# Block-causal attention and a feed-forward layer on one core: the last query and key blocks turned in the PSUM bank of the scores

## The chip, the cores and the metric

The kernel runs on one core of a Trainium2 chip. Its engines are TensorE (PE in the profile, with its weight loads as PEld), VectorE (DVE), ScalarE (ACT), GpSimd (POOL) and SyncE (SP, which here only issues DMAs). Each engine works through its own instructions in order, and they wait for each other through semaphores. The metric is the device time of one launch in microseconds; the time shown is a median of three runs.

## The reference

Attention over 8 batches of 8 heads with 576 positions of 64 columns each. A query may look at keys of its own block of 64 and of earlier blocks. The heads of a batch are then put side by side as rows of 512 columns, and a feed-forward layer with a clipped quadratic in its middle follows. All tensors are float32.

```
scores = scale * np.matmul(q, k.transpose(0, 1, 3, 2))
mask = block_i >= block_j                  # blocks of 64 positions
scores = np.where(mask, scores, -1000000000.0)
attn = np.exp(scores - np.max(scores, axis=-1, keepdims=True))
attn = attn / (np.sum(attn, axis=-1, keepdims=True) + 1e-09)
attn_out = np.matmul(attn, v)

x = attn_out.transpose(0, 2, 1, 3).reshape(B * S, H * D)     # 4608 x 512
h = x @ w_in                                                  # 512 x 2048
g = np.where(h >= 1, h, np.where(h <= -1, 0.0, (h + 1) ** 2 / 4))
out = g @ w_out
```

## The kernel before, in words

Every product is made of float32r words: each operand is split into a high and a low word, and the products of words are summed in PSUM.

**Attention** goes by pairs of heads (`Pair`, 32 of them, four per batch). A head has 4.5 tiles of 128 queries: tiles 0 to 3 and a last block of 64. The last blocks of the two heads of a pair are handled together. For a head `j`, `scores(j, 0)` does query tiles 0 and 1, `scores(j, 1)` tile 2 (128 queries by 384 keys) and `scores(j, 2)` tile 3 (by 512 keys); `scores_last` does the last block of both heads. Each of these multiplies on TensorE (L484 and L487), takes the maximum of a row on VectorE (L508), the exponential on ScalarE (L513, with a read of the row sums behind it), then the sum plus a small number, the reciprocal and the scaling on VectorE (L494, L495, L519). The scaled tile `pr` then goes through a DMA into `prr` (L251), is transposed on TensorE (`turn`, L559) and split into two words by ScalarE and VectorE (L552, L554). `attn_v` multiplies with the values (L598), `add_words` adds its two halves with ScalarE and VectorE (L620, L621), and `store_x` writes the rows for the feed-forward layer (L663, L664).

From batch 2 on (`raw`, 24 pairs) queries and keys are loaded as they are and transposed together: `turned_raw` for tiles 0 to 3 of one head (L403), `turned_last` for the last blocks of both heads (L444). `parted` then makes the words: ScalarE writes the high words of the queries (L390), VectorE the low ones (L391), ScalarE those of the keys (L396), VectorE the rest (L397). `turned_last` copies the blocks to `qa` and `ka` by two more VectorE instructions (L448).

**The feed-forward layer** is interleaved, one half step after each of the eight steps of a pair: `ffn_in` has 12 matmuls of 512 columns into one PSUM bank `ph` (L777), then ScalarE (L786), VectorE (L787, L790), ScalarE (L791) and GpSimd (L792); `ffn_out` has 12 matmuls with the other weights (L801, L806).

**PSUM.** There are eight banks: four for the sums `po`, one for `ph` and three that `work_bank` hands out in turn to everything else. In the pairs from batch 2 on there are 22 such requests a pair, so a bank is used again at the third request after it, and its next writer waits until its last reader is done. The requests around the change are `scores(0, 0)`, `attn_v_first`, `turn(1, 2)` of the pair before, `scores(0, 1)`, `turned_last`, `attn_v(1)` of the pair before, `scores(0, 2)`, `turn(0, 0)` and the two banks of `scores_last`. `turned_last` thus gets the bank that `attn_v_first` had, whose last reader is the second L621 of that step.

The order on each engine is laid down when the program is built, by a scheduler that keeps close to the order of the code but may let instructions of different engines' queues pass each other.

Of the kernel before, what the change touches and what calls it, by code (L numbers as in the profile page):

```python
# [9 lines left out]
F32R = mybir.dt.float32r  # L10
# [13 lines left out]
def block_attn_then_ffn(  # L24
# [9 lines left out]
    nc = tc.nc  # L34
    B, H, S, D = q.shape
    NT, DM = out.shape
    DF = w_in.shape[1]
    P = 128
    BLK = 64
    NTL = S // P  # L40
# [5 lines left out]
    TCH = 512  # L46
# [5 lines left out]
    SCALE = 1.0 / float(D) ** 0.5  # L52
# [25 lines left out]
    def work_bank(name):  # L78

        banks["n"] += 1  # L80
        if banks["free"] and banks["n"] % 2:
            return ps_o.tile([P, 512], F32, tag="po", name=name)
        return ps_w.tile([P, 512], F32, tag="work", name=name)
# [4 lines left out]
    ident_r = const.tile([P, P], F32R, tag="ident", name="ident_r")  # L88
# [13 lines left out]
    qa = const.tile([P, 2, QW], F32R, tag="qa", name="qa")  # L102
    qb = const.tile([P, 2, QW], F32R, tag="qb", name="qb")
    ka = const.tile([P, 2, S], F32R, tag="ka", name="ka")
    kb = const.tile([P, 2, S], F32R, tag="kb", name="kb")

    def last_blocks(t_):

        view = t_[:, :, SM : SM + BLK]
        if t_.shape[2] == S:  # L110
            return view
        part, (_, two), cols = view.ap
        return bass.AP(tensor=view.tensor, offset=view.offset, ap=[part, [QW + BLK, two], cols])
# [120 lines left out]
    def as_float32r(src, plain):  # L234

        if plain:
            wide = src.shape[1] > RING - 2 * S
            places = SPARE_WIDE if wide else SPARE
            moved = [places[spare[wide] % len(places)]]
            spare[wide] += 1  # L240
            if src.shape[1] > TCH:
                if "end" not in spare:
                    spare["end"] = att1.tile([P, G0 + P], F32R, tag="pa11", name="pre")[:, :BLK]
                moved.append(spare["end"])
            for i, dst in enumerate(moved):
                n = min(TCH, src.shape[1] - i * TCH)
                nc.sync.dma_start(dst[:, :n].bitcast(F32), src[:, i * TCH : i * TCH + n])
            return moved
        n, moved = src.shape[1], []
        wide = wide_tile(F32R, "prr")  # L250
        nc.sync.dma_start(wide[:, :n].bitcast(F32), src)  # L251
        for c0 in range(0, n, TCH):
            moved.append(wide[:, c0 : min(c0 + TCH, n)])
        return moved


    class Pair:
# [157 lines left out]
        def turned(self, is_q, j):  # L415
# [18 lines left out]
            else:  # L434
                nc.sync.dma_start(
                    a[:D, j, :SM].bitcast(F32), bt[hi0 : hi0 + D, j, :SM].bitcast(F32)
                )

        def turned_last(self):

            ps = work_bank("ps_qk")
            if self.raw:
                ps = ps[:, :P]
                nc.tensor.transpose(ps.bitcast(F32R), self.qk[:, 2 * NTL, :, :], ident_r)  # L444
                ps = ps.rearrange("p (h c) -> p h c", h=2)
                self.parted(last_blocks, ps)
                for i, a in enumerate((qa, ka)):
                    nc.vector.tensor_scalar_mul(  # L448
                        last_blocks(a)[:D], ps[i * D : (i + 1) * D], 1.0 if i else SCALE
                    )  # L450
                return
            for i, src in enumerate((self.qs, self.ks)):
                nc.tensor.transpose(
                    ps[:, i * P : (i + 1) * P].bitcast(F32R), src[:, 2 * NTL, :, :], ident_r
                )
            for i, (a, bt, hi0) in enumerate(((qa, qb, 0), (ka, kb, D))):
                blocks = ps[:, i * P : (i + 1) * P].rearrange("p (h c) -> p h c", h=2)
                nc.scalar.copy(last_blocks(bt), blocks)
                nc.vector.tensor_copy(last_blocks(a)[:D], blocks[hi0 : hi0 + D])
# [34 lines left out]
                nc.vector.tensor_scalar_add(total[:, i : i + 1], total[:, i : i + 1], EPS)  # L494
            nc.vector.reciprocal(total, total)  # L495

        def scores(self, j, g):
            tiles = self.GROUPS[g]
            m = len(tiles)
            ps = work_bank("ps_s")  # L500
            pr = att3.tile([P, S], F32, tag="pr", name="pr")
            nm = small.tile([P, 2], F32, tag="nm", name="nm")
            sm = small.tile([P, 2], F32, tag="sm", name="sm")
            cols = [slice(at, at + (t + 1) * P) for t, at in tiles]
            for (t, _), cs in zip(tiles, cols):
                self.product(ps[:, cs], j, t * P, 0, (t + 1) * P, True, True)
            for i, cs in enumerate(cols):
                nc.vector.tensor_reduce(  # L508
                    out=nm[:, i : i + 1], in_=ps[:, cs], axis=AX.X, op=ALU.max, negate=True
                )  # L510
            raw = ps if self.b < AT_HOME else pr
            for i, cs in enumerate(cols):
                nc.scalar.activation(  # L513
                    raw[:, cs], ps[:, cs], AF.Exp, bias=nm[:, i : i + 1], scale=1.0,
                    accum_out=sm[:, i : i + 1],
                )
            self.inverse(sm[:, :m])
            for i, cs in enumerate(cols):
                nc.vector.tensor_scalar_mul(pr[:, cs], raw[:, cs], sm[:, i : i + 1])  # L519
            self.pr[j, g] = as_float32r(pr[:, : cols[-1].stop], self.plain) if self.hop else [pr]  # L520
# [149 lines left out]
    def attention_steps():  # L670

        pairs = [Pair(b, hp) for b in range(B) for hp in range(NPAIR)]
        first = pairs[0]
        first.load_qk()
        first.split_q()
        first.split_k()
        first.turned(True, 0)
        first.turned(False, 0)
        first.turned(True, 1)
        old = None  # L680
        for i, cur in enumerate(pairs + [None]):
            nxt = pairs[i + 1] if i + 1 < len(pairs) else None
            far = old is not None and old.far
            near = old is not None and not old.far
            if far:
                old.turn(1, 1)
            if cur:
                cur.scores(0, 0)
                cur.turned(False, 1)
                cur.load("v")  # L690
            if far:
                old.attn_v_first()
            if near:
                old.turn(1, 2)
            yield
            if far:
                old.turn(1, 2)
            if cur:
                cur.scores(0, 1)
                cur.turned_last()  # L700
            if i + 2 < len(pairs):
                pairs[i + 2].fetch()
            if near:
                old.attn_v(1)
                old.store_x()
            yield
            if far:
                old.attn_v(1)
                old.store_x()
            if not cur:  # L710
                return
            if cur.far:
                cur.scores(0, 2)
            else:
                cur.begin()
                cur.scores(0, 2)
                cur.turn(0, 0)
            yield
            if cur.far:
                cur.begin()  # L720
                cur.turn(0, 0)
                cur.scores_last()
            else:
                cur.scores_last()
                cur.turn(0, 1)
            if nxt:
                nxt.load_qk()
                nxt.split_q()
            yield
            if nxt:  # L730
                nxt.split_k()
            if cur.far:
                cur.turn(0, 1)
                cur.scores(1, 0)
            else:
                cur.scores(1, 0)
                cur.turn(0, 2)
            if nxt:
                nxt.turned(True, 0)
            yield  # L740
            if cur.far:
                cur.turn(0, 2)
                cur.scores(1, 1)
            else:
                cur.scores(1, 1)
                cur.turn_last()
            if nxt:
                nxt.turned(False, 0)
            yield
            if cur.far:  # L750
                cur.turn_last()
                cur.scores(1, 2)
            else:
                cur.scores(1, 2)
                cur.attn_v(0)
                cur.turn(1, 0)
            yield
            if cur.far:
                cur.turn(1, 0)
                cur.attn_v(0)  # L760
            else:
                cur.turn(1, 1)
                cur.attn_v_first()
            if nxt:
                nxt.turned(True, 1)
            yield
            old = cur
# [124 lines left out]
```

## Time and profile before

| | |
|---|---|
| median of 3 runs | 1239.24 us (1237.13 to 1243.8) |
| profiled execution | 1239.06 us, of which 1237.3 us is the span from the first to the last instruction |
| PE busy | 1186.6 us (96%), 6280 matmuls |
| DVE busy | 863.8 us (70%) |
| ACT busy | 698.5 us (56%) |
| POOL busy | 371.8 us (30%) |
| chain that ended last | PE 86%, DVE 5%, DMA 4%, ACT 2%, issue 2% |
| turned blocks, L444 | 24 matmuls, 5.9 us, from 259.1 to 1016.5 us |

The pairs that the change touches run from about 259 us to about 1050 us. A row of the timeline has the start in microseconds from the span's start, the duration, the engine, the line of the code, the operation, what it writes and reads, the shape, and, where the engine was idle before, for how long and what ended it. Matmuls overlap in the rows: what one costs is the distance of the starts.

### The profile page before, as it was taken

The numbers are of one execution on the slowest core, as the hardware profiler recorded it, in microseconds if no ns is written. First come the engines' busy times: TensorE is split into PE (matmuls) and PEld (weight loads), VectorE is DVE, ScalarE is ACT, GpSimd is POOL, SyncE is SP. The second block draws the span as 40 slices with busy tenths as digits, with TensorE's granted clock in tenths as the row PEclk, the third lists the DMA queues.
The fourth block names the chain that finished last, engine by engine and source line by source line (L and its number), as shares of the span: only waits on it lengthen the run. The fifth ranks groups of instructions, "written<-read, shape, count | busy, mean of one in ns | idle before, by whom it ended". The sixth has DMA issues, their size and how long they took to land.

```text
span 1237.3 us, 19822 instructions
## 1 busy us (share of the span) xinstructions
PE 1186.6 (96%) x6280; PEld 993.1 (80%) x6280; DVE 863.8 (70%) x2124; ACT 698.5 (56%) x1731; POOL 371.8 (30%) x366
## 2 busy tenths in 40 slices
PE   4878898999999999999999999999999999999998
PEld 3666677788888888888888888888888888888886
DVE  8888778658777877787777877787778776322322
ACT  5877667546566656665666665666566654222222
POOL 3444546312222222222222222222222222222222
PEclk9988998999999999999999999999999999999999
DMA  5756776778986655565555555565556443333332
GB/s 165 213 176 208 235 247 221 225 202 255 291 270 219 192 162 156 147 198 166 163 159 180 164 160 160 148 196 151 155 149 192 142 135 111 119 102 102 120 103 102
DMA packets 177192, 215.40 MB, mean 174 GB/s; under 512 B 109872, under 2 KB 128304, under 8 KB 176320
## 3 DMA queue, kind: packets, MB, share of 16 engines
q1 hardware_dynamic: 177088, 214.14, 56.1%
q8 instruction: 50, 0.82, 0.3%
q14 instruction: 54, 0.44, 0.1%
HBM read 134.74 MB, written 31.98 MB: 135 GB/s over the span
## 4 chain that ended last, share of the span: by engine, by line
PE 86%; DVE 5%; DMA 4%; ACT 2%; issue 2%; POOL 1%; SPq 0%; ACTq 0%; DVEq 0%; POOLq 0%
PE ph L777 31%; PE po L801 20%; PE po L806 10%; PE ps_av L598 9%; PE ps_s L484 5%; PE ps_s L487 4%; PE ps_t L559 4%; PE ps_qk L403 1%; DMA bits<-in_moe_w_in_dram 1%; DVE bits L172 1%; POOL bits L184 1%; PE ps_t L561 1%; DVE nm L508 1%; DVE bits L178 1%; DVE shifted L175 1%
## 5 line engine op out<-in xcount | busy, mean ns | idle before, releaser
L792 POOL TENSOR_TENSOR gl<-t,gh 128x512 fp32r<-128x512 f32 x144 | 186.5, 1295 | 522.8 <-ACT gh L791 338.2
L801 PE MATMUL po<-wo,gh 128*128 128x512 f32 x1152 | 294.1, 396 | 0.1
L801 PEld LDWEIGHTS po<-wo,gh 128*128 128x128 f32 x1152 | 211.2, 188 | 43.3 <-ACT gh L791 0.6
L777 PE MATMUL ph<-xh,wih 128*128 128x512 f32 x576 | 232.7, 404 | 0.4 <-DVE t L790 0.4
L777 PE MATMUL ph<-xh,wil 128*128 128x512 f32 x576 | 228.1, 396 | 0.0
L777 PE MATMUL ph<-xl,wih 128*128 128x512 f32 x576 | 226.9, 394 | 0.0
L787 DVE SCALAR_TENSOR_TENSOR t<-t 128x512 f32<-128x512 f32 x144 | 101.0, 701 | 161.5 <-ACT t L786 158.6
L786 ACT ACTIVATE t<-ph 128x512 f32<-128x512 f32 x144 | 86.2, 599 | 160.5 <-PE ph L777 160.5
L791 ACT CAST gh<-t 128x512 fp32r<-128x512 f32 x144 | 89.4, 621 | 118.9 <-DVE t L790 118.8
L806 PE MATMUL po<-wo,gl 128*128 128x512 f32 x576 | 155.3, 391 | 0.0
L484 PE MATMUL ps_s<-ka,qa 68*128 68x288 f32 (+4 forms) x384 | 133.8, 363 | 4.9 <-DMA ka<-mrow 4.0
L513 ACT ACTIVATE pr<-ps_s,nm 128x128 f32<-128x128 f32 x192 | 100.4, 525 | 57.5 <-DVE nm L508 56.4
L508 DVE TENSOR_REDUCE nm<-ps_s 128x1 f32<-128x128 f32 (+3 forms) x256 | 118.9, 482 | 16.4 <-PE ps_s L487 15.6
L777 PEld LDWEIGHTS ph<-xh,wil 128*128 128x128 f32 x576 | 109.1, 189 | 24.0
L806 PEld LDWEIGHTS po<-wo,gl 128*128 128x128 f32 x576 | 108.0, 188 | 22.9
L777 PEld LDWEIGHTS ph<-xl,wih 128*128 128x128 f32 x576 | 109.6, 190 | 19.3
L777 PEld LDWEIGHTS ph<-xh,wih 128*128 128x128 f32 x576 | 109.2, 190 | 19.3 <-DVE t L790 0.8
L381 POOL TENSOR_TENSOR vsr<-vn,vsr 64x64 fp32r<-64x64 f32 (+1 forms) x96 | 56.5, 589 | 227.1 <-ACT vsr L380 226.0
L487 PE MATMUL ps_s<-kb,qb 128*128 128x288 f32 (+4 forms) x384 | 120.4, 321 | 0.0
L790 DVE TENSOR_TENSOR t<-ph,t 128x512 f32<-128x512 f32 x144 | 98.7, 685 | 2.0
L559 PEld LDWEIGHTS ps_t<-ident_r,prr 128*128 128x128 f32 x600 | 68.5, 139 | 22.4 <-issue 0.5
L494 DVE TENSOR_SCALAR sm<-sm 128x1 f32<-128x1 f32 x256 | 38.5, 151 | 65.0 <-ACT pr L513 54.8
(115 smaller groups left out, 1879.7 us busy)
## 6 DMA issues: line engine op xcount, KB each, us to landing
wo<-wo_split SPq DMA_DIRECT2D x144, 512.0 KB, 3.4
prr<-pr SPq DMA_DIRECT2D x96, 192.0 KB, 3.0
prr<-pr SPq DMA_DIRECT2D x48, 256.0 KB, 2.8
out_dram<-ob SPq DMA_DIRECT2D x36, 256.0 KB, 2.9
bits<-in_moe_w_in_dram SPq DMA_DIRECT2D x16, 512.0 KB, 4.6
bits<-in_moe_w_out_dram SPq DMA_DIRECT2D x16, 512.0 KB, 4.0
wo_split<-ws SPq DMA_DIRECT2D x16, 512.0 KB, 2.9
qa<-qb SPq DMA_DIRECT2D x63, 128.0 KB, 2.4
```

The costliest lines, as they stand in the source:

```text
L484: nc.tensor.matmul(ps, qa[:KA, j, c0 : c0 + P], ka[:KA, j, k0 : k0 + n], start=first, stop=False)
L487: nc.tensor.matmul(ps, qb[:, j, c0 : c0 + P], kb[:, j, k0 : k0 + n], start=False, stop=last)
L508: nc.vector.tensor_reduce(out=nm[:, i : i + 1], in_=ps[:, cs], axis=AX.X, op=ALU.max, negate=True)
L513: nc.scalar.activation(raw[:, cs], ps[:, cs], AF.Exp, bias=nm[:, i : i + 1], scale=1.0, accum_out=sm[:, i : i + 1],)
L559: nc.tensor.transpose(out.bitcast(F32R), src, ident_r)
L598: nc.tensor.matmul(ps[:, lo_col:], vt, x, start=first and i == 0 and m == 0, stop=last and i == len(parts) - 1 and m == len(mov) - 1,)
L777: nc.tensor.matmul(ph, w[:, cc, fs], x[:, cc, xs], start=(cc == 0 and i == 0), stop=(cc == NCC - 1 and i == 2),)
L787: nc.vector.scalar_tensor_tensor(out=t_, in0=t_, scalar=1.0, in1=t_, op0=ALU.min, op1=ALU.mult)
L790: nc.vector.tensor_tensor(out=t_, in0=ph, in1=t_, op=ALU.max)
L792: nc.gpsimd.tensor_tensor(out=gl, in0=t_, in1=gh.bitcast(F32), op=ALU.subtract)
L801: nc.tensor.matmul(po[tt], gh[:, ts_], wo[:, w, :], start=(fc == 0 and w == 0), stop=False)
L806: nc.tensor.matmul(po[tt], gl[:, ts_], wo[:, 0, :], start=False, stop=fc == NFC - 1)
```

## The change

`turned_last` of the pairs from batch 2 on no longer asks for a bank. The transposition (`turn_raw_last`) is put ahead of the two matmuls of `scores(0, 1)`, into columns 384 to 511 of the same bank, which this 384-column product leaves free. The instructions that read the turned blocks (`part_raw_last`) are put between the maximum and the exponential of `scores(0, 1)`. What is computed stays the same.

```diff
+        def turn_raw_last(self, ps):
+            nc.tensor.transpose(ps.bitcast(F32R), self.qk[:, 2 * NTL, :, :], ident_r)
+
+        def part_raw_last(self, ps):
+            ps = ps.rearrange("p (h c) -> p h c", h=2)
+            self.parted(last_blocks, ps)
+            for i, a in enumerate((qa, ka)):
+                nc.vector.tensor_scalar_mul(
+                    last_blocks(a)[:D], ps[i * D : (i + 1) * D], 1.0 if i else SCALE
+                )
+
         def turned_last(self):
 
+            if self.raw:
+                return
             ps = work_bank("ps_qk")
-            if self.raw:
-                ps = ps[:, :P]
-                nc.tensor.transpose(ps.bitcast(F32R), self.qk[:, 2 * NTL, :, :], ident_r)
...
-                return
...
-        def scores(self, j, g):
+        def scores(self, j, g, last=False):
...
             ps = work_bank("ps_s")
+            if last:
+                self.turn_raw_last(ps[:, TCH - P :])
...
                 nc.vector.tensor_reduce(
                     out=nm[:, i : i + 1], in_=ps[:, cs], axis=AX.X, op=ALU.max, negate=True
                 )
+            if last:
+                self.part_raw_last(ps[:, TCH - P :])
             raw = ps if self.b < AT_HOME else pr
...
-                cur.scores(0, 1)
+                cur.scores(0, 1, cur.raw)
                 cur.turned_last()
```

The lines behind the change are 3 to 7 higher in the new kernel: L484 becomes L487, L487 becomes L490, L508 L513, L513 L520, L519 L526, L786 L793. Three places show what moves; all are from one pair of heads in the middle of the program, and the other pairs from batch 2 on are alike.

On TensorE, between the transposes of `turn(1, 2)` and the next `ffn_in`, there stood before:

```order
L559 MATMUL ps_t<-ident_r,prr 128x128 x3
L484 MATMUL ps_s<-ka,qa 128x384 [waits Activation_49]
L487 MATMUL ps_s<-kb,qb 128x384
L444 MATMUL ps_qk<-ident_r,qk 128x128 [waits DVE_49,PE_49]
L777 MATMUL ph<-xh,wih 128x512
```

and now:

```order
L566 MATMUL ps_t<-ident_r,prr 128x128 x3
L440 MATMUL ps_s<-ident_r,qk 128x128 [waits Activation_49]
L487 MATMUL ps_s<-ka,qa 128x384
L490 MATMUL ps_s<-kb,qb 128x384
L784 MATMUL ph<-xh,wih 128x512 [waits DVE_49]
```

The transposition stands two rows earlier, and the wait for a bank that VectorE has to free is gone from it.

On ScalarE, from the first instruction on the turned blocks to `scores_last`, there stood before:

```order
L390 ACTIVATE qb<-ps_qk 64x2x64 [waits PE_49]
L513 ACTIVATE pr,sm<-ps_s,nm 128x384 [waits DMAHW1_49,DVE_49]
L396 CAST kb<-ps_qk 64x2x64 [waits DVE_49]
L786 ACTIVATE t<-ph 128x512 [waits PE_49,Pool_49]
L380 CAST vsr_109<-vn 128x4x64 [waits PE_49]
L620 COPY xtmp<-ps_av 64x320 [waits PE_49,Activation_49]
L791 CAST gh<-t 128x512 [waits DVE_49]
L380 CAST vsr_109<-vn 64x64
L513 ACTIVATE pr,sm<-ps_s,nm 128x512 [waits DMAHW3_49,DVE_49]
L663 CAST xh<-x_6660 128x576 [waits DVE_49]
```

and now:

```order
L390 ACTIVATE qb<-ps_s 64x2x64 [waits DVE_49]
L396 CAST kb<-ps_s 64x2x64 [waits DVE_49]
L520 ACTIVATE pr,sm<-ps_s,nm 128x384 [waits DMAHW1_49,DVE_49]
L793 ACTIVATE t<-ph 128x512 [waits PE_49,Pool_49]
L380 CAST vsr_109<-vn 128x4x64 [waits PE_49]
L627 COPY xtmp<-ps_av 64x320 [waits PE_49,Activation_49]
L380 CAST vsr_109<-vn 64x64
L798 CAST gh<-t 128x512 [waits DVE_49]
L670 CAST xh<-x_6650 128x576 [waits DVE_49]
L520 ACTIVATE pr,sm<-ps_s,nm 128x512 [waits DMAHW3_49,DVE_49]
```

Both instructions on the turned blocks stand ahead of the exponential of the 384-column tile and wait for VectorE, and the exponential of the 512-column tile stands behind the cast to `xh`.

On VectorE, from the maximum of the 384-column tile to that of the 512-column tile, there stood before:

```order
L508 TENSOR_REDUCE nm<-ps_s 128x1 [waits PE_49]
L554 TENSOR_TENSOR pb_6659<-ps_t,pb_6658 128x4x128 [waits Activation_49]
L391 SCALAR_TENSOR_TENSOR qb<-ps_qk,qb 64x2x64 [waits Activation_49]
L494 TENSOR_SCALAR sm<-sm 128x1 [waits Activation_49]
L495 RECIPROCAL sm<-sm 128x1 [waits DVE_49]
L519 TENSOR_SCALAR pr<-pr,sm 128x384 [waits DMAHW1_49,DVE_49]
L397 TENSOR_TENSOR kb<-ps_qk,kb 64x2x64 [waits Activation_49]
L448 TENSOR_SCALAR qa<-ps_qk 64x2x64
L448 TENSOR_SCALAR ka<-ps_qk 64x2x64
L787 SCALAR_TENSOR_TENSOR t<-t 128x512 [waits Activation_49]
L790 TENSOR_TENSOR t<-ph,t 128x512 [waits DVE_49]
L508 TENSOR_REDUCE nm<-ps_s 128x1 [waits PE_49]
```

and now:

```order
L391 SCALAR_TENSOR_TENSOR qb<-ps_s,qb 64x2x64 [waits Activation_49]
L397 TENSOR_TENSOR kb<-ps_s,kb 64x2x64 [waits Activation_49]
L446 TENSOR_SCALAR qa<-ps_s 64x2x64
L446 TENSOR_SCALAR ka<-ps_s 64x2x64
L497 TENSOR_SCALAR sm<-sm 128x1 [waits Activation_49]
L498 RECIPROCAL sm<-sm 128x1 [waits DVE_49]
L526 TENSOR_SCALAR pr<-pr,sm 128x384 [waits DMAHW1_49,DVE_49]
L794 SCALAR_TENSOR_TENSOR t<-t 128x512 [waits Activation_49]
L797 TENSOR_TENSOR t<-ph,t 128x512 [waits DVE_49]
L628 TENSOR_TENSOR x_6650<-ps_av,xtmp 64x320 [waits Activation_49]
L513 TENSOR_REDUCE nm<-ps_s 128x1 [waits PE_49]
```

The four instructions on the turned blocks stand together ahead of the sum, the reciprocal and the scaling of the 384-column tile, and `add_words` (L628) passes ahead of the maximum of the 512-column tile. On SP the DMA of the scaled 384-column tile to `prr` stands four rows later than before, behind loads of the next pair's queries and keys.

More of the change, by code (lines that the diff above doesn't have):

```diff
@@ L437, in turned @@
                 )
+        def turn_raw_last(self, ps):
[7 more added lines that the diff above has]
+                )
         def turned_last(self):
+            if self.raw:
+                return
             ps = work_bank("ps_qk")
-            if self.raw:
-                ps = ps[:, :P]
[L444 to L450, printed above, removed]
-                return
             for i, src in enumerate((self.qs, self.ks)):
```

## The prediction

> **What bounds the kernel now.** I read the busy time by stretches first. In the middle of the pairs that the change touches the columns are PE, PEld, DVE, ACT and POOL, each with its instruction count, then the granted clock:
>
> ```profile
> 500.00:700.00 200.00, 199.74 (x1113) 169.97 (x1112) 156.11 (x392) 123.02 (x316) 54.95 (x57) 1.00 0.56 168
> ```
>
> PE is busy throughout, 199.74 of 200 us, at the full clock (1.00). DVE is busy for 156 us of it. So time can only come from places where matmuls stand further apart than they must, and DVE is the engine with the least room behind. The waits of the weight loads name one such place:
>
> ```profile
> PEld ps_qk L444 <- PE ps_s L487: 5.9, 17, 0.4
> ```
>
> Before the transposition of the last blocks the weight load stood idle 17 times, up to 0.4 us. This is PE there, in a pair with the wait, then in one without, and at the other head's `scores(1, 1)`, where no transposition follows:
>
> ```profile
> 589.75 0.46 PE L559 MATMUL ps_t<-ident_r,prr 128*128 128x128 f32 x4
> 590.04 0.41 PE L484 MATMUL ps_s<-ka,qa 68*128 68x384 f32 x1
> 590.29 0.34 PE L487 MATMUL ps_s<-kb,qb 128*128 128x384 f32 x1
> 590.69 0.25 PE L444 MATMUL ps_qk<-ident_r,qk 128*128 128x128 f32 x1
> ...
> 591.08 0.39 PE L777 MATMUL ph<-xl,wih 128*128 128x512 f32 x1
> ```
> ```profile
> 426.75 0.35 PE L487 MATMUL ps_s<-kb,qb 128*128 128x384 f32 x1
> 426.94 0.22 PE L444 MATMUL ps_qk<-ident_r,qk 128*128 128x128 f32 x1
> ...
> 427.31 0.39 PE L777 MATMUL ph<-xl,wih 128*128 128x512 f32 x1
> ```
> ```profile
> 606.64 0.34 PE L487 MATMUL ps_s<-kb,qb 128*128 128x384 f32 x1
> ...
> 607.05 0.40 PE L777 MATMUL ph<-xl,wih 128*128 128x512 f32 x1
> ```
>
> From L487 to L444 PE takes 0.40 us in the first and 0.19 us in the second. The view names L487 as releaser, yet at 426.94 L444 starts while L487 (426.75 + 0.35) still runs, so it needn't wait for that. What it waits for is the bank: its last reader is the second L621, which ends at 590.12 + 0.43 = 590.55, just ahead of 590.69 (row in the next block).
>
> **The change, part by part.**
>
> *TensorE.* From L487 to the second L777 it is 0.79 us with the wait, 0.56 us without it, and 0.41 us where no transposition stands between. The moved transposition joins a row of like ones, which stand (590.04 - 589.75) / 4 = 0.07 us apart. So PE could save 0.79 - 0.41 - 0.07 = 0.31 us in 17 pairs and 0.56 - 0.48 = 0.08 us in the other 7: 5.3 + 0.6 = **5.9 us**. The wait that the transposition takes over (ScalarE, the exponential of `scores(0, 0)`) held L484 at the same place before, so it adds nothing. This is all there is to win, if nothing behind it gets late.
>
> *VectorE and ScalarE.* Here the exponential of the 384-column tile now stands behind six instructions on the turned blocks, which go back and forth between two engines. The rows of one pair, VectorE and then ScalarE:
>
> ```profile
> 590.12 0.43 DVE L621 TENSOR_TENSOR x<-ps_av,xtmp 64x256 f32<-64x256 f32 x1
> ...
> 591.15 0.56 DVE L508 TENSOR_REDUCE nm<-ps_s 128x1 f32<-128x384 f32 x1
> ...
> 592.34 0.29 DVE L391 SCALAR_TENSOR_TENSOR qb<-ps_qk,qb 64x128 fp32r<-64x128 f32 x1
> ...
> 593.05 0.42 DVE L519 TENSOR_SCALAR pr<-pr,sm 128x384 f32<-128x384 f32 x1
> 593.50 0.29 DVE L397 TENSOR_TENSOR kb<-ps_qk,kb 64x128 fp32r<-64x128 f32 x1
> 593.81 0.28 DVE L448 TENSOR_SCALAR qa<-ps_qk 64x128 fp32r<-64x128 f32 x1
> 594.10 0.29 DVE L448 TENSOR_SCALAR ka<-ps_qk 64x128 fp32r<-64x128 f32 x1
> 594.46 0.69 DVE L787 SCALAR_TENSOR_TENSOR t<-t 128x512 f32<-128x512 f32 x1
> 595.18 0.69 DVE L790 TENSOR_TENSOR t<-ph,t 128x512 f32<-128x512 f32 x1
> 595.79 0.68 DVE L508 TENSOR_REDUCE nm<-ps_s 128x1 f32<-128x512 f32 x1
> 596.50 0.49 DVE L621 TENSOR_TENSOR x<-ps_av,xtmp 64x320 f32<-64x320 f32 x1
> ...
> 597.77 0.49 DVE L519 TENSOR_SCALAR pr<-pr,sm 128x512 f32<-128x512 f32 x1
> 599.02 0.56 DVE L554 TENSOR_TENSOR pa<-ps_t,pa 128x384 fp32r<-128x384 f32 x1 [0.76 <-ACT pa L552]
> 599.50 0.81 DVE L533 TENSOR_REDUCE nm<-ps_s 128x1 f32<-128x288 f32 x2
> ...
> 602.10 0.52 DVE L548 TENSOR_SCALAR pr<-pr,sm 128x576 f32<-128x576 f32 x1
> 603.06 0.69 DVE L787 SCALAR_TENSOR_TENSOR t<-t 128x512 f32<-128x512 f32 x1 [0.45 <-ACT t L786]
> ```
> ```profile
> 590.98 0.27 ACT L390 ACTIVATE qb<-ps_qk 64x128 fp32r<-64x128 f32 x1
> 591.75 0.58 ACT L513 ACTIVATE pr<-ps_s,nm 128x384 f32<-128x384 f32 x1 [0.50 <-DVE nm L508]
> 592.23 0.20 ACT L513 ACTIVATION_READ_ACCUMULATOR pr<-ps_s,nm 128x1 f32 x1
> 592.66 0.26 ACT L396 CAST kb<-ps_qk 64x128 fp32r<-64x128 f32 x1 [0.24 <-DVE qb L391]
> ...
> 596.58 0.68 ACT L513 ACTIVATE pr<-ps_s,nm 128x512 f32<-128x512 f32 x1
> 597.17 0.19 ACT L513 ACTIVATION_READ_ACCUMULATOR pr<-ps_s,nm 128x1 f32 x1
> ...
> 600.54 0.50 ACT L539 ACTIVATE pr<-ps_s,nm 128x288 f32<-128x288 f32 x1 [1.55 <-DVE nm L537]
> ...
> 601.42 0.20 ACT L539 ACTIVATION_READ_ACCUMULATOR pr<-ps_s,nm 128x1 f32 x1
> ```
>
> I follow the new order through these durations, under the old line numbers. Between dependent instructions lie 0.03 to 0.04 us (591.15 + 0.56 to 591.75); where nothing is waited for and the shapes are alike, the next starts about 0.08 us before the end (595.18 + 0.69 = 595.87, L508 at 595.79).
>
> 1. Up to the maximum DVE is never idle from 590.12 on, so PE being earlier does not move it: it ends at 591.71. L390 now waits for it, 591.75 to 592.02, beside DVE's L554. L391 stays at 592.34 and L396 at 592.66 to 592.92.
> 2. Then L397 (0.29), L448 (0.28) and L448 (0.29), with 0.01 us between the L448s as before: 592.96 to 593.85. Only now the exponential: 593.89, and its sums are read 0.48 us later, to 594.57. Before that was 592.43, so it is **2.14 us late**.
> 3. L519 starts 0.41 us after such a read (597.36 to 597.77): 594.98 to 595.40. L787, which no longer waits for ScalarE's L786, runs from 595.32 to 596.01, L790 from 596.04 to 596.73, L621 from 596.76 to 597.25, the maximum of the 512-column tile from 597.28 to 597.96.
> 4. Its exponential starts at 598.00 and the sums are read to 598.78 (0.59 + 0.19 us), instead of 597.36: **1.42 us late**.
>
> Who waits for it? The second bank of `scores_last` is the one that `scores(0, 2)` had three requests before, as in the old kernel. Its first weight load is this row:
>
> ```profile
> 598.78 0.19 PEld L484 LDWEIGHTS ps_s<-ka,qa 68*128 68x128 f32 x1
> ```
>
> Before, the exponential was done 1.42 us ahead of it. Now PE, 0.31 us earlier, wants to load at 598.47, and is let go at 598.78 + 0.04 = 598.82. So it waits 0.35 us there, and stands **0.04 us behind** the old kernel. In the pairs like that at 426 it comes out the same:
>
> ```profile
> 426.33 0.43 DVE L621 TENSOR_TENSOR x<-ps_av,xtmp 64x256 f32<-64x256 f32 x1
> ```
>
> There the second L777 (427.31) stands 0.55 us behind this L621's end (426.76), in the pair at 590 0.53 us (591.08 and 590.55): PE is as far ahead of VectorE in both, so the chain is as late for it.
>
> 5. From there: L519 599.19 to 599.68, L554 (0.56) from 599.60, the two maxima (0.81) from 600.08 to 600.89. The exponential follows 0.23 us after them as before (600.31 to 600.54), its last read ends 1.08 us after that start, at 602.20. L548 starts 0.48 us later and ends at 603.20. L787 then starts at 603.12 at the earliest; its other input, L786, is 0.04 us later with PE, which gives 603.10. These meet within 0.02 us. So the work that leads to `scores(1, 1)` (L487 at 606.64) is 0.04 to 0.06 us late, PE as well, and the next pair begins in the same state.
>
> **Sum:** 23 pairs (the first, with another `attn_v`, I leave out) by 0.04 us, +0.9 us. Against the profiled 1239.06 us that is 1240.0 us; against the median of the runs, which lies 0.2 us higher, **1240.2 us**. Bounds: nothing of step 4 late gives -5.9 us; each tenth of a microsecond more in the chain gives +2.3 us, since its cover of 1.42 us is used up.
>
> *What else moves.* On SP the DMA of the 384-column tile goes behind four loads of queries and keys, issued while it waits for DVE anyway.
>
> ```profile
> prr<-pr SPq DMA_DIRECT2D x96, 192.0 KB, 3.0
> 602.18 0.29 PE L559 MATMUL ps_t<-ident_r,prr 128*128 128x128 f32 x2
> ```
>
> Ready at 595.40, it lands by 598.5 after 3.0 us, and is transposed at 602.18: 3.7 us of cover, without which each microsecond would cost one per pair. The three loads behind it wait about a microsecond, for the next pair. `attn_v(1)` now waits for the bank that L621 frees at 590.55, some 3 us ahead of it. The cast L791 and with it POOL's L792 come 0.9 us later, for an `ffn_out` that comes a whole step later.
>
> *A page against the row.* At 591.75 the exponential waits for the other engine's maximum on its bank, and the new order makes it wait for the last L448 in the same way, though that reads other columns. The Trainium skill, PSUM — Partial Sum Buffer, section PSUM bank collisions raise a hardware error, has it that two engines must keep apart in a bank and quadrant of 32 partitions, whatever the columns, but may use different quadrants of a bank at once. By that, L396 (partitions 64 to 127) need not wait for L391 (0 to 63), and the chain would be 0.30 us shorter, 23 x 0.26 = 6.0 us off the sum. The built program has that wait (the rows of the order), so I take it as it is.
>
> **The rivals.** (a) *The saving stays*: the chain to the 512-column exponential is over 0.3 us shorter than I add up, because instructions of 64 partitions overlap as well. For it: PE's wait surely goes. Against it: L391 starts 0.03 us after L554's end and L397 0.03 us after L519's, never earlier. It gives 1239.2 - 5.9 = 1233.3 us. (b) *DVE becomes the bound*: the new neighbours do not overlap. The start of L787 then costs 0.11 us at step 3, and L554, both maxima and the second L787 0.11 us each at step 5. From the moment that L548 ends after 603.18, where L786's result comes, DVE and no longer PE sets `scores(1, 1)`: 0.04 + 0.11 a pair if only step 3 is hit (1242.7 us), 0.04 + 0.55 if all are (1252.8 us). Against it: like neighbours of these shapes overlap at 595.79 and, as the 0.81 us for two maxima show, at 599.50. (c) *The change does nothing*, as L444's wait was not the bank's: 1239.2 us; the pair at 426 speaks against it.
>
> **How the numbers follow.** Forecast, with the chain right to within 0.1 us a pair (1238 to 1243 us): 0.60. (a), whole or in part: 0.17. (b): 0.20, half of it above 1246 us. (c): 0.03. The range runs from (a)'s 1233.0 to 1247.0 us and leaves out the upper half of (b). About 0.5% (6.2 us) is what a measurement can tell from no change. (a) lies at the edge of it: 0.08 faster. (b) above 1245.4 us and some scatter: 0.15 slower. The same: 0.77.
>
> **What would show it.** L440 without idle time before it; the exponential of the 384-column tile at about 2.1 us after the end of its maximum; the 512-column one's read ending about 8.2 us after the second L621 of 256 columns; and a new wait of PE of about 0.3 us at the second bank of `scores_last`, for ScalarE's exponential. If PE waits at `scores(1, 1)` instead, (b) is right; if it waits nowhere, (a).

## The result, and the profile after

| | before | after |
|---|---|---|
| median of 4 runs | 1238.97 us (1237.13 to 1243.8) | 1254.8 us (1251.95 to 1256.3) |
| span of the profiled execution | 1237.3 us | 1254.5 us |

The ratio of the means is 1.012, with a 95% interval of 1.0094 to 1.0146: the changed kernel is 1.2% **slower**, by 15.8 us of the medians. The forecast was 1240.2 us, no change, and the time lies above the range. Line numbers are now those of the changed kernel (L519 is L526, L533 is L540, L548 is L555, L554 is L561, L621 is L628, L663 and L664 are L670 and L671, L787 is L794, L791 and L792 are L798 and L799).

The busy time by stretches, with the columns of before (PE, PEld, DVE, ACT, POOL), for the same 200 us of the changed kernel:

```profile
500.00:700.00 200.00, 196.91 (x1087) 166.53 (x1086) 156.91 (x386) 118.75 (x310) 54.57 (x54) 1.00 0.55 164
```

PE did 1087 matmuls there instead of 1113, at the same full clock, and stood idle for 3 us instead of 0.3. DVE is as busy as before (156.91 us to 156.11) for less work done. The page's chain of work that ended last says where PE's idle time comes from:

```profile
PE 54%; DVE 25%; ACT 9%; issue 6%; DMA 4%; POOL 1%; SPq 1%; ACTq 0%; DVEq 0%; POOLq 0%
```

PE had 86% of it before and DVE 5%. The weight loads' waits, before and after, name the place where PE meets it:

```profile
PEld ps_s L484 <- ACT pr L513: 2.2, 6, 0.4
```
```profile
PEld ps_s L487 <- ACT pr L520: 18.7, 46, 0.6
```

The wait of L444 is gone. In its place, a matmul of scores waits 46 times for an exponential, 18.7 us in all, where it waited 6 times before. One pair from the timeline, first TensorE around the moved transposition (L440):

```profile
631.83 0.46 PE L566 MATMUL ps_t<-ident_r,prr 128*128 128x128 f32 x4
632.12 0.25 PE L440 MATMUL ps_s<-ident_r,qk 128*128 128x128 f32 x1
632.20 0.41 PE L487 MATMUL ps_s<-ka,qa 68*128 68x384 f32 x1
```

L440 follows the four transposes at their own distance, (632.12 - 631.83) / 4 = 0.07 us apart, and has no idle time. Then VectorE and ScalarE of the same pair, from the second L628 of 256 columns to the scaling of the last block:

```profile
632.21 0.43 DVE L628 TENSOR_TENSOR x<-ps_av,xtmp 64x256 f32<-64x256 f32 x1
...
633.25 0.56 DVE L513 TENSOR_REDUCE nm<-ps_s 128x1 f32<-128x384 f32 x1
...
634.44 0.28 DVE L391 SCALAR_TENSOR_TENSOR qb<-ps_s,qb 64x128 fp32r<-64x128 f32 x1
635.05 0.29 DVE L397 TENSOR_TENSOR kb<-ps_s,kb 64x128 fp32r<-64x128 f32 x1 [0.33 <-ACT kb L396]
...
637.07 0.42 DVE L526 TENSOR_SCALAR pr<-pr,sm 128x384 f32<-128x384 f32 x1
637.41 0.68 DVE L794 SCALAR_TENSOR_TENSOR t<-t 128x512 f32<-128x512 f32 x1
...
639.37 0.69 DVE L513 TENSOR_REDUCE nm<-ps_s 128x1 f32<-128x512 f32 x1
...
641.30 1.27 DVE L526 TENSOR_SCALAR pr<-pr,sm 128x512 f32<-128x512 f32 x1
642.49 0.55 DVE L561 TENSOR_TENSOR pa<-ps_t,pa 128x384 fp32r<-128x384 f32 x1
642.95 0.81 DVE L540 TENSOR_REDUCE nm<-ps_s 128x1 f32<-128x288 f32 x2
...
645.55 0.52 DVE L555 TENSOR_SCALAR pr<-pr,sm 128x576 f32<-128x576 f32 x1
```
```profile
634.76 0.26 ACT L396 CAST kb<-ps_s 64x128 fp32r<-64x128 f32 x1 [0.64 <-DVE qb L391]
635.98 0.58 ACT L520 ACTIVATE pr<-ps_s,nm 128x384 f32<-128x384 f32 x1 [0.96 <-DVE ka L446]
...
639.38 0.68 ACT L670 CAST xh<-x 128x576 fp32r<-128x576 f32 x1
640.10 0.69 ACT L520 ACTIVATE pr<-ps_s,nm 128x512 f32<-128x512 f32 x1
640.69 0.19 ACT L520 ACTIVATION_READ_ACCUMULATOR pr<-ps_s,nm 128x1 f32 x1
```

One row is out of line: the scaling of the 512-column tile at 641.30 takes **1.27 us**, where the same instruction took 0.49 us at 597.77 before. It is the same shape, and the engine did not wait ahead of it. Over the whole program the groups by line and shape say it once more (the instructions, then busy time and mean ns), before and after:

```profile
L519 DVE TENSOR_SCALAR pr<-pr,sm 128x512 f32<-128x512 f32 x48 | 29.9, 624 | 1.7
```
```profile
L526 DVE TENSOR_SCALAR pr<-pr,sm 128x512 f32<-128x512 f32 x48 | 44.3, 922 | 1.7
```

48 instructions became 14.4 us longer in all; no other group of VectorE changed by more than 3 us. What else ran at that moment shows in GpSimd's timeline, here at 597.77 in the kernel before and at 641.30 in the changed one:

```profile
596.67 1.30 POOL L792 TENSOR_TENSOR gl<-t,gh 128x512 fp32r<-128x512 f32 x1 [0.60 <-ACT vsr L380]
597.93 0.51 POOL L381 TENSOR_TENSOR vsr<-vn,vsr 64x64 fp32r<-64x64 f32 x1
598.40 1.42 POOL L664 TENSOR_TENSOR xl<-x,xh 128x576 fp32r<-128x576 f32 x1
```
```profile
639.61 1.29 POOL L799 TENSOR_TENSOR gl<-t,gh 128x512 fp32r<-128x512 f32 x1 [0.64 <-ACT gh L798]
640.86 1.42 POOL L671 TENSOR_TENSOR xl<-x,xh 128x576 fp32r<-128x576 f32 x1
```

Before, the subtraction of `store_x` (L664) started 0.14 us after the scaling's end (598.40 and 598.26). Now its cast (L670) stands ahead of the exponential of the 512-column tile and the small L381 ahead of L799, so the subtraction (L671) starts as soon as L799 is done, 0.44 us ahead of the scaling, and ends at 642.28; the scaling ends at 642.57, 0.29 us later. PE's weight loads stand idle twice in the pair. The first time, at the second bank of `scores_last`, is ahead of the scaling and is the wait that was forecast. The second time, at `scores(1, 1)`, comes behind the scaling, which has made all that leads there late:

```profile
640.93 0.19 PEld L487 LDWEIGHTS ps_s<-ka,qa 68*128 68x128 f32 x1 [0.28 <-ACT pr L520]
...
649.26 0.19 PEld L487 LDWEIGHTS ps_s<-ka,qa 68*128 68x128 f32 x1 [0.60 <-ACT pr L520]
```

To measure the pairs alone, without what comes ahead of them, I take the time from the scaling of head 0's 512-column tile in the first pair of batch 2 to that of head 1's in the 22nd: 44 scalings, 21.5 pairs. The two ends, before and after:

```profile
270.08 0.49 DVE L519 TENSOR_SCALAR pr<-pr,sm 128x512 f32<-128x512 f32 x1
...
975.09 0.48 DVE L519 TENSOR_SCALAR pr<-pr,sm 128x512 f32<-128x512 f32 x1
```
```profile
273.19 0.49 DVE L526 TENSOR_SCALAR pr<-pr,sm 128x512 f32<-128x512 f32 x1
...
991.24 0.49 DVE L526 TENSOR_SCALAR pr<-pr,sm 128x512 f32<-128x512 f32 x1
```

This stretch takes 705.01 us before and 718.05 us after, **13.0 us** more. In it 21 scalings of head 0 became longer: 13 took 1.27 us, 0.78 more, and 8 took 0.86 us, 0.37 more (there `store_x` meets the end of a ring and its subtraction comes in two pieces, of 384 and 192 columns; the scaling waits only for the one of 384, which takes 1.01 us). That is 10.1 + 3.0 = 13.1 us, all of it.

### The profile page after: what moved, and what is told of

It is laid out like the page before. It is cut to its first block, busy times and chain, and to the rows that moved or that the text cites. A ratio compares the mean times of both kernels' runs of the same rounds, so it can differ in the third digit from the quotient of the medians.

```text
span 1254.5 us, 19809 instructions
## 1 busy us (share of the span) xinstructions
PE 1196.6 (95%) x6280; PEld 999.3 (80%) x6280; DVE 873.7 (70%) x2124; ACT 693.1 (55%) x1731; POOL 378.6 (30%) x366
## 4 chain that ended last, share of the span: by engine, by line
PE 54%; DVE 25%; ACT 9%; issue 6%; DMA 4%; POOL 1%; SPq 1%; ACTq 0%; DVEq 0%; POOLq 0%
PE ph L784 24%; PE po L808 11%; PE ps_av L605 6%; PE po L813 5%; ACT pr L520 4%; DVE nm L513 3%; DVE t L794 3%; DVE t L797 3%; PE ps_s L487 3%; DVE pr L526 3%; DVE pb L561 2%; PE ps_t L566 2%; PE ps_s L490 2%; DVE pr L555 1%; DVE x L628 1%
## 5 line engine op out<-in xcount | busy, mean ns | idle before, releaser
L799 POOL TENSOR_TENSOR gl<-t,gh 128x512 fp32r<-128x512 f32 x144 | 186.2, 1293 | 531.1 <-ACT gh L798 334.9
L794 DVE SCALAR_TENSOR_TENSOR t<-t 128x512 f32<-128x512 f32 x144 | 100.6, 699 | 148.2 <-ACT t L793 147.5
L798 ACT CAST gh<-t 128x512 fp32r<-128x512 f32 x144 | 89.4, 621 | 139.6 <-DVE t L797 139.5
L793 ACT ACTIVATE t<-ph 128x512 f32<-128x512 f32 x144 | 85.9, 597 | 118.1 <-PE ph L784 118.1
L487 PE MATMUL ps_s<-ka,qa 68*128 68x288 f32 (+4 forms) x384 | 137.3, 371 | 13.5 <-ACT pr L520 8.4
L520 ACT ACTIVATE pr<-ps_s,nm 128x128 f32<-128x128 f32 x192 | 100.6, 526 | 71.4 <-DVE nm L513 46.2
L513 DVE TENSOR_REDUCE nm<-ps_s 128x1 f32<-128x128 f32 (+3 forms) x256 | 118.9, 482 | 18.1 <-PE ps_s L490 16.6
L381 POOL TENSOR_TENSOR vsr<-vn,vsr 64x64 fp32r<-64x64 f32 (+1 forms) x96 | 61.0, 645 | 228.5 <-ACT vsr L380 227.1
L490 PE MATMUL ps_s<-kb,qb 128*128 128x288 f32 (+4 forms) x384 | 121.4, 322 | 0.0
L487 PEld LDWEIGHTS ps_s<-ka,qa 68*128 68x128 f32 x384 | 74.5, 194 | 26.5 <-ACT pr L520 18.7
```

Source lines behind the costliest of these rows:

```text
L487: nc.tensor.matmul(ps, qa[:KA, j, c0 : c0 + P], ka[:KA, j, k0 : k0 + n], start=first, stop=False)
L490: nc.tensor.matmul(ps, qb[:, j, c0 : c0 + P], kb[:, j, k0 : k0 + n], start=False, stop=last)
L513: nc.vector.tensor_reduce(out=nm[:, i : i + 1], in_=ps[:, cs], axis=AX.X, op=ALU.max, negate=True)
L520: nc.scalar.activation(raw[:, cs], ps[:, cs], AF.Exp, bias=nm[:, i : i + 1], scale=1.0, accum_out=sm[:, i : i + 1],)
L793: nc.scalar.activation(t_, ph, AF.Relu, bias=0.5, scale=0.5)
L794: nc.vector.scalar_tensor_tensor(out=t_, in0=t_, scalar=1.0, in1=t_, op0=ALU.min, op1=ALU.mult)
```

## The experiments

**Theory A**: the change itself costs next to nothing, as forecast, and the 15 us are the meeting of that scaling with GpSimd's subtraction. **Theory B**: the chain on VectorE is too long by itself, as in rival (b), and the meeting only lies beside it. The change itself is compared with the 1238.97 us above, the experiments with the kernel before on their own chip: 1238.46 us for the first four, 1241.02 us for the last three. The ratio is again that of the means. The last column is the stretch above.

| run | median us (range) | ratio, 95% interval | stretch, us |
|---|---|---|---|
| the change as it is | 1254.8 (1251.95 to 1256.3) | 1.012 [1.0094, 1.0146] | 718.05 |
| e1_split_sub | 1240.45 (1235.22 to 1241.74) | 1.0007 [0.9992, 1.0022] | 705.17 |
| e2_part_after_exp | 1233.22 (1232.62 to 1235.31) | 0.9957 [0.9941, 0.9973] | 699.63 |
| e3_scalar_first | 1246.81 (1244.99 to 1249.05) | 1.0065 [1.0047, 1.0083] | 711.63 |
| e4_after_exp_scalar_first | 1233.19 (1232.07 to 1234.85) | 0.9955 [0.9939, 0.9971] | 699.61 |
| e5_before_split | 1238.62 (1236.1 to 1244.47) | 0.9993 [0.9977, 1.001] | 705.40 |
| e6_after_exp_split | 1231.94 (1230.5 to 1233.87) | 0.9937 [0.9921, 0.9953] | 699.65 |
| e7_after_exp_split_both | 1234.03 (1231.97 to 1235.32) | 0.9953 [0.9936, 0.9969] | 700.55 |

### e1: GpSimd's subtraction in three pieces

The changed kernel, with nothing moved but the subtraction of `store_x` cut into pieces of 192 columns:

```diff
-                nc.gpsimd.tensor_tensor(
-                    out=xl[:, self.hp, at : at + n], in0=self.x32[:, c0 : c0 + n],
-                    in1=hi.bitcast(F32), op=ALU.subtract,
-                )
+                for p0 in range(0, n, 192):
+                    nc.gpsimd.tensor_tensor(
+                        out=xl[:, self.hp, at + p0 : at + p0 + 192],
+                        in0=self.x32[:, c0 + p0 : c0 + p0 + 192],
+                        in1=hi[:, p0 : p0 + 192].bitcast(F32), op=ALU.subtract,
+                    )
```

> The changed kernel, with GpSimd's subtraction of store_x cut into pieces of 192 columns; the order on the other engines stays. Theory A (VectorE's scaling of the 512-column tile stands still until GpSimd's running subtraction is done, and then needs 0.28 us more): the pieces take about 0.5 us, so the scaling takes 0.49 us in every pair instead of 0.86 to 1.27, a pair comes back from 33.1 to 33.5 us to about 32.7, and the kernel to 1238 to 1243 us. Theory B (the chain of VectorE and ScalarE is longer because the new neighbours do not overlap, and the scaling is only one of many): the scaling may take 0.49 us, but the kernel stays above 1248 us, with PE still waiting at scores(1, 1).

It took 1240.45 us, and the stretch is 0.16 us from that of before. The timeline of this kernel at the scaling, DVE and then POOL:

```profile
632.94 0.49 DVE L526 TENSOR_SCALAR pr<-pr,sm 128x512 f32<-128x512 f32 x1
```
```profile
632.51 1.94 POOL L672 TENSOR_TENSOR xl<-x,xh 128x192 fp32r<-128x192 f32 x3
```

GpSimd starts as far ahead of the scaling as in the changed kernel (0.43 us), but VectorE gets in behind the first piece and takes 0.49 us. GpSimd's three pieces take 1.94 us instead of 1.42. Over the whole program, the waits of the weight loads for this exponential and the group of the scaling are now:

```profile
PEld ps_s L487 <- ACT pr L520: 6.9, 23, 0.4
```
```profile
L526 DVE TENSOR_SCALAR pr<-pr,sm 128x512 f32<-128x512 f32 x48 | 29.7, 619 | 1.7
```

Of the 46 waits 23 are left: 17 of 0.27 to 0.30 us at the second bank of `scores_last`, as forecast, and 6 of 0.34 to 0.39 us, one in every fourth pair, like the 6 before. The 22 waits at `scores(1, 1)`, which B needs, are gone. So the meeting was about 14 us of the 15.8, and A holds: TensorE's saving and the late chain together come to nothing that can be measured.

### e2: the readers of the turned blocks behind the exponential

The changed kernel, with `part_raw_last` behind the loop of the exponential:

```diff
-            if last:
-                self.part_raw_last(ps[:, TCH - P :])
             raw = ps if self.b < AT_HOME else pr
...
+            if last:
+                self.part_raw_last(ps[:, TCH - P :])
```

> The changed kernel, with the reading of the turned blocks moved behind the exponential of the same tile. Theory A: the exponential of the 384-column tile is back at 0.04 us after its maximum, that of the 512-column tile stands ahead of the cast to xh again, the scaling of the 512-column tile takes 0.49 us, and PE keeps what the transposition's place saves: 0.31 us in the pairs that waited, 1232 to 1235 us. Theory B says the same of the exponential, but has PE wait elsewhere for VectorE: 1237 to 1241 us. If the wait at the transposition was not for the bank, no gain: 1239 us.

1233.22 us: **faster than both kernels**, by 0.4% against the one before. The stretch is 5.4 us shorter than before, and the prediction's saving of TensorE, 5.9 us in 24 pairs, would be 5.3 us in 21.5. The timeline of this kernel at the scaling, DVE and then POOL:

```profile
595.22 0.49 DVE L526 TENSOR_SCALAR pr<-pr,sm 128x512 f32<-128x512 f32 x1
```
```profile
594.12 1.30 POOL L799 TENSOR_TENSOR gl<-t,gh 128x512 fp32r<-128x512 f32 x1 [0.92 <-ACT vsr L380]
595.37 0.52 POOL L381 TENSOR_TENSOR vsr<-vn,vsr 64x64 fp32r<-64x64 f32 x1
595.86 1.42 POOL L671 TENSOR_TENSOR xl<-x,xh 128x576 fp32r<-128x576 f32 x1
```

The subtraction starts after the scaling's end again (595.71), and the order around it is that of before.

### e3 and e4: ScalarE's two instructions first

The changed kernel (e3) and e2 (e4), with the words of the turned blocks made in another order, so that L396 no longer waits for L391:

```diff
-            self.parted(last_blocks, ps)
+            qhi, qlo = last_blocks(qb[:D]), last_blocks(qb[D:])
+            klo, khi = last_blocks(kb[:D]), last_blocks(kb[D:])
+            nc.scalar.mul(qhi, ps[:D], SCALE)
+            nc.scalar.copy(khi, ps[D:])
+            nc.vector.scalar_tensor_tensor(
...
+            nc.vector.tensor_tensor(out=klo, in0=ps[D:], in1=khi.bitcast(F32), op=ALU.subtract)
```

> The changed kernel, with both of ScalarE's instructions on the turned blocks ahead of VectorE's four, so that the cast of the keys no longer waits for VectorE. The chain to the exponential of the 384-column tile gets 0.3 us shorter (the cast runs beside VectorE's subtraction of 512 columns). Theory A: all behind it moves up by 0.3 us, GpSimd's subtraction too, so the collision stays (scaling 0.86 to 1.27 us): about 23 x 0.3 = 7 us less, 1246 to 1250 us. Theory B: as many microseconds less, but PE's wait at scores(1, 1) is what shrinks and the scaling has no part in it.

> Both edits together: turned blocks read behind the exponential, ScalarE's two instructions first. Theory A: the cast of the keys was hidden in the second experiment already, so within 2 us of it, 1232 to 1236 us. Theory B: another few microseconds less, since the chain is shorter.

In e3 the second product on VectorE follows the first without a gap (its timeline; L448 is L391, L452 is L397):

```profile
631.02 0.28 DVE L448 SCALAR_TENSOR_TENSOR qb<-ps_s,qb 64x128 fp32r<-64x128 f32 x1
631.32 0.29 DVE L452 TENSOR_TENSOR kb<-ps_s,kb 64x128 fp32r<-64x128 f32 x1
...
637.57 1.28 DVE L534 TENSOR_SCALAR pr<-pr,sm 128x512 f32<-128x512 f32 x1
```

They start 0.30 us apart instead of 0.61, and the stretch is 718.05 - 711.63 = 6.4 us shorter, 0.30 us a pair. The scaling still takes 1.28 us: PE waits for the chain here, so the 0.30 us counts in full, but the meeting stays. In e4, where the chain has room, the same edit gives nothing (699.61 and 699.63 us).

### e5 and e6: the cut where nothing meets

The same cut in the kernel before (e5) and in e2 (e6), to see whether it is a gain by itself.

> The kernel before, with the subtraction of store_x on GpSimd cut into pieces of 192 columns as in the run on the changed kernel. Theory A (what the change cost is that it moved this subtraction onto the scaling of the 512-column tile): in the kernel before the two do not meet (the scalings of this tile there run beside L792, and take 0.49 us but for six of 1.52 us), so the cut gains nothing: 1237 to 1241 us, and the scalings stay at a mean of 0.62 us. Theory B (cutting the instruction is a gain by itself, because VectorE gets in between pieces at many places, and the 14 us of the earlier run were that and not the change undone): 1222 to 1232 us.

> The changed kernel with part_raw_last behind the exponential of the 384-column tile (1233.2 us by itself) and with the subtraction of store_x in pieces of 192 columns. Theory A: the late subtraction does not meet the scaling in that order either (mean of the 48 scalings 0.62 us), so the cut adds nothing: 1231 to 1236 us. Theory B (the cut is a gain by itself): under 1228 us.

It is not: in e5 1238.62 us and a stretch of 705.40 us (705.01 without the cut), in e6 1231.94 us and 699.65 us (699.63). So what e1 took away is what the change had brought. e6 has the lowest median of all, but its stretch does not tell it from e2.

### e7: the other subtraction in two pieces as well

e6, with the subtraction L792 of the feed-forward half step in two pieces of 256 columns:

```diff
-        nc.gpsimd.tensor_tensor(out=gl, in0=t_, in1=gh.bitcast(F32), op=ALU.subtract)
+        for p0 in range(0, 512, 256):
+            pc = slice(p0, p0 + 256)
+            nc.gpsimd.tensor_tensor(
+                out=gl[:, pc], in0=t_[:, pc], in1=gh[:, pc].bitcast(F32), op=ALU.subtract
+            )
```

> As the run before, and also the subtraction of the feed-forward half step on GpSimd (gl, 512 columns) in two pieces of 256. Six scalings of the 512-column tile, one in every fourth pair, take 1.52 us because that subtraction starts 0.04 us ahead of them. Theory A: with pieces each of these takes about 1.0 us at most, and if the pairs around it stay bound by TensorE nothing else changes: 1229 to 1234 us, the long scalings shorter by some 0.5 us. Rival: the second piece makes GpSimd's work on each half step some 0.2 to 0.3 us longer and puts it onto other VectorE instructions: 1236 us or more.

Its timeline, for head 1 of a fourth pair and head 0 of the second pair behind it:

```profile
548.98 0.97 DVE L526 TENSOR_SCALAR pr<-pr,sm 128x512 f32<-128x512 f32 x1
...
597.24 0.62 DVE L526 TENSOR_SCALAR pr<-pr,sm 128x512 f32<-128x512 f32 x1
```

The long scalings went from 1.52 to 0.97 us, as expected. But those of head 0 went from 0.49 to 0.62 us, since GpSimd's two pieces end later, and the stretch is 0.9 us longer than e6's. The time, 1234.03 us, lies a hair above the 1229 to 1234 us that A expected and below the rival's 1236 us: the rival's mechanism is there, its size is not, and there is no gain.

## Why the prediction was wrong

*TensorE's saving: right.* L440 has no idle time, and e2 gets the 5.4 us where 5.3 were worked out.

*Steps 1 to 4: right, to 0.02 us.* Measured from the end of the second L628 (632.64) and set against the prediction's times from 590.55: the exponential of 384 columns starts 3.34 us after it (3.34), the scaling of 384 columns 4.43 (4.43), the maximum of 512 columns 6.73 (6.73), its exponential 7.46 (7.45), and the read ends 8.24 us after it (8.23). PE waits 0.28 us at the second bank of `scores_last`, where 0.35 was worked out (in 17 pairs; in every fourth pair it does not wait there).

*Step 5: here it failed.* "L519 599.19 to 599.68" is the term: 0.49 us for the scaling of the 512-column tile, as in the row at 597.77. It started on time, 8.66 us after L628 (8.64), and took 1.27 us in 13 of the 21 pairs of the stretch and 0.86 us in 8. The scaling of the last block then ends 13.43 us after L628 where 12.65 was forecast, late by the same 0.78 us. Since step 4 had used up all of the cover, as the prediction said, every tenth of it went into the sum.

Under "what else moves" GpSimd's work was looked at for who waits for its result, and not for what it runs beside. The meeting could have been read from the prediction's own numbers. L792 comes 0.9 us later, so it ends at 596.67 + 1.30 + 0.9 = 598.87. The order of ScalarE that is shown with the change has the `xh` cast ahead of the exponential of the 512-column tile, so it is done by 598.00. It also has the small cast L380, which feeds the small L381, ahead of the cast L791, so L381 need not stand between L792 and the subtraction any more. The subtraction behind L792 then starts at about 598.87, 0.3 us ahead of the scaling at 599.19, and lasts 1.42 us. And the trace of before held the price. There a scaling like it, in every fourth pair, met L792 (timeline of before, DVE and then POOL):

```profile
549.45 1.52 DVE L519 TENSOR_SCALAR pr<-pr,sm 128x512 f32<-128x512 f32 x1
```
```profile
549.40 1.28 POOL L792 TENSOR_TENSOR gl<-t,gh 128x512 fp32r<-128x512 f32 x1 [8.06 <-ACT gh L791]
```

1.52 us there, 0.49 us at 597.77: the group's mean of 624 ns was the sign that one form has two durations. The Trainium skill has the rule, in SBUF — State Buffer, section Who interferes with whom: VectorE and GpSimd share a pair of ports as an exclusive lock, a tensor_scalar in a two-port mode needs it, and whoever issues first keeps it for the whole instruction. Both kernels' rows agree that the scaling waits: 0.49 us without GpSimd, 1.27 and 1.52 us behind it. No row shows the mode or the ports themselves.

*The sum.* Without this term it was right: e1 took 1240.45 us, and the forecast was 1240.2.

*The rivals.* (b) named the right place and the right sign, PE waiting at `scores(1, 1)`, and that DVE would set it from a few hundredths on. But its mechanism, neighbours that do not overlap, is not what happened: L794 starts 0.08 us ahead of the end of the scaling before it (637.41 and 637.49) and the two maxima still take 0.81 us. That its upper price, 1252.8 us, lies near the measured time is chance. (a) needed a shorter chain, and the chain was as long as added up; e2 reaches its time, 1233 us, by another order. (c) is out, since e2 keeps the saving.

*The rule of the Trainium skill that the prediction weighed* (PSUM — Partial Sum Buffer, section PSUM bank collisions raise a hardware error) would not make L396 wait for L391, which the prediction put at 6.0 us off. The program does have that wait (0.64 us idle at 634.76), and taking it away by the order of the code was worth 6.4 us in e3's stretch. So the size was about right. But in e3 VectorE starts on the bank at 631.02, after ScalarE's cast of the keys has ended at 630.97, so it is not shown that two engines can use one bank at the same time.

*What is not settled.* Of the 15.8 us of the medians, the stretch explains 13.0 us and the two pairs behind it another 1.2 us (66.09 us from the stretch's end to the last of the 48 scalings, 64.86 us before). The last 1.6 us are within the interval of the ratio (11.6 to 18.1 us; the means differ by 14.7 us); the nine traces begin the stretch anywhere between 269.06 and 273.19 us, and what makes that differ was not looked into.

## What to carry to other kernels

When a change moves an instruction, follow what it releases on every engine, down to GpSimd, and ask of each not only who waits for it but which VectorE instruction it will run beside; a group whose mean lies off its usual duration (624 ns against 490) shows that such meetings have a price here. A change that uses up all of a chain's cover (here 1.42 us late under a cover of 1.42 us) pays in full for whatever else it brings into that chain. Try instructions that share a bank behind the reader that the chain waits for, not only ahead of it: here this one move turned 1254.8 us into 1233.2 us, as it shortened the chain and took the meeting away.

## What the hardware showed

**A scaling waits out GpSimd and 0.28 us more.** In all nine traces the 512-column scaling from SBUF (48 in each) takes, to within 0.01 us, the larger of 0.49 us and what is left of GpSimd's instruction plus 0.28 us: 0.98 us left gives 1.27, 1.24 gives 1.52, 0.57 gives 0.86, and in e7 0.34 gives 0.62. Up to 0.20 us left costs nothing. (Each trace is one execution, and the profile calls its spans on GpSimd rough.)

**The same scaling from PSUM does not wait.** In batches 0 and 1 it reads the scores from PSUM. Its 16 instances take 746 ns on average. Nine of them start while GpSimd works, with 0.27 to 1.30 us of its instruction left, and none of these takes more than 0.75 us. One of them (timeline of the changed kernel, DVE and then POOL):

```profile
33.66 0.75 DVE L526 TENSOR_SCALAR pr<-ps_s,sm 128x512 f32<-128x512 f32 x1
```
```profile
33.43 1.30 POOL L188 TENSOR_TENSOR wil<-bits,wih 128x512 fp32r<-128x512 f32 x1 [0.84 <-DVE sm L497]
```

GpSimd had 1.07 us left when it started. So the form that is 0.26 us slower alone is the faster one where 0.98 us or more of GpSimd's instruction is left (0.75 us against 1.27); a version that scales from PSUM in this place was not tried.
